# Every matmul of the inner loop on 64x32 tiles of the array, row halves summed on VectorE, and two score slots for three

## The chip, the core and the metric

The kernel runs on one core of a Trainium2 chip. The metric is the device time in microseconds; a kernel's time is the median of its runs. Beside the timed runs one execution was profiled, and all durations below come from that one.

The engines are PE (TensorE, matrix products; PEld is its loading of weights), DVE (VectorE), ACT (ScalarE), POOL (GpSimd) and SP (which here issues most DMAs). Each works through its own list of instructions in order and waits for the others by semaphores.

## The reference

Two attention layers read the same input and are mixed by a gate. Layer A has 32 query heads over one shared head of keys and values; layer B has 32 full heads. Sequence 2048, model width 512, head width 16, all float32.

```python
g = _sigmoid((x * gate_w).sum(-1, keepdims=True))
# A: q = x@wq in 32 heads; k = x@wk, v = x@wv (one head)
# B: q, k, v = x@wqkv in 32 heads each
scores = einsum("bhqd,bhkd->bhqk", q, k) * (Dh ** -0.5)   # A: "bhqd,bkd->bhqk"
p = _softmax(scores, axis=-1)
o = einsum("bhqk,bhkd->bhqd", p, v)                        # A: "bhqk,bkd->bhqd"
layer = o.transpose(...).reshape(B, S, D) @ wo
return g * a + (1 - g) * b
```

## The kernel before, in words

**Groups and blocks.** The heads are taken in eight groups of eight heads, A and B in turn. A group has two halves of 1024 queries. A half has four passes `s`; a pass treats four blocks at once (two heads by two query blocks of 512) and runs over 16 key chunks `c` of 128. One block of one chunk is a 128x512 tile of scores, keys on the rows. One step of the main loop is one chunk of one pass: four blocks. There are 1024 steps and 2048 activations, each over two blocks.

**A step.** `scores(u)` makes two blocks on PE into one slot of two PSUM banks (`sc`, three slots), fp16 operands split into high and low parts stacked on 64 rows, so each block is a 64x128 tile of the array and two run side by side. ACT takes the exponential of the 128x1024 slot into `pr`. `values(m)` multiplies `pr` with the values (float32, 128x32 tiles, four blocks side by side on the four column strips) and sums over the 16 chunks in one PSUM bank `aux[turn]`. A column of ones beside the values gives the softmax denominators. A float32 product shows as two matmuls in the trace. After chunk 15 the bank is copied to `raw` by DVE, DMAs spread it into `oT` (sums) and `dT` (denominators), the turn flips, and the other bank of `aux` takes the next pass.

**Side work.** The bank that is not being summed into (`aux[1 - turn]`) serves for all other products, in parts that are slipped into the steps: projections of the next groups' queries and keys (`project`, units of 12 parts; a part is one `by_tiles` call, four matmuls 128*32 over 512 columns), B's values (`v_units`), and the output projection (`o_unit`, three parts for 128 rows of output, added into `acc` by DVE with the gate). `norm_task` (called "a norm" below) divides 128 columns of `oT` by `dT` on DVE: reciprocal, multiplication, and the split into two fp16 parts. Before the loop x is turned and split, and the first projections are made.

**The order.** All instructions are written out by this program, with no scheduler behind it. `_Tasks` decides when side work is issued: `step` runs parts at a rate worked out from each unit's due time, at most about two per step, and issues at most one side function (a norm, a load) per step. In the list of a step stand both `scores`, then `values` of two steps before, then the parts:

```python
for u in range(STEP * j // ACT, STEP * (j + 1) // ACT):
    scores(u)
if j >= 2:
    values(j - 2)
```

Of the kernel before, what the change touches and what calls it, by code (L numbers as in the profile page):

```python
# [10 lines left out]
F32 = mybir.dt.float32  # L11
# [7 lines left out]
P = 128  # L19
# [8 lines left out]
ACT = 2  # L28
STEP = 4
COLS = 32  # L30
SCALE = DH ** -0.5
# [30 lines left out]
class _Tasks:  # L62
# [3 lines left out]
    def __init__(self):  # L66
        self.now, self.credit, self.rest = 0, 0.0, 0
        self.units, self.open, self.side = [], deque(), deque()
        self.moves, self.moved = deque(), 0
# [11 lines left out]
    def _run(self, left):  # L81
        if not self.open:
            for u in self.units:
                if u[0] <= self.now and self.rest <= self.now and len(u[2]) <= 2 * (left - 1):
                    self.units.remove(u)
                    self.open.extend(u[2])
                    break
        if not self.open:
            return False
        self.open.popleft()()  # L90
        if not self.open:
            self.rest = self.now + 1
        return True

    def step(self, left):
        self.now += 1
        if self.side and self.side[0][0] <= self.now and len(self.open) not in (1, 2):
            self.side.popleft()[1]()
        if self.moves and self.moved <= self.now - 3:
            self.moved = self.now  # L100
            self.moves.popleft()()
        n = len(self.open)
        rate = n / max(1, left - 1)
        for u in self.units:
            n += len(u[2]) + 1
            rate = max(rate, n / max(1, u[1] - self.now))
        self.credit = min(self.credit + rate, 2.2)
        while self.credit >= 1.0 and self._run(left):
            self.credit -= 1.0

    def finish(self):
        while self.open:
            self.open.popleft()()
        self.rest = self.now + 1

    def flush(self):

        assert not self.moves
        self.rest = 0
        ahead = 0  # L120
        while self.open or self.units or self.side:
            if self.side and ahead < 2 and not (self.units and not ahead):
                self.side.popleft()[1]()
                ahead += 1
                continue
            ahead -= ahead > 0
            self.now += 100
            self._run(1 << 20)
            self.finish()
            self.rest = 0  # L130

# [10 lines left out]
def _fast(ctx, tc, x, wq_a, wk_a, wv_a, wo_a, wqkv_b, wo_b, gate_w, out, flag):  # L142
# [11 lines left out]
    turn = [0]  # L154

    xT = cst.tile([P, 2, NK, S], F16, name="xT")
# [11 lines left out]

    def by_tiles(out, lhsT, rhs, start, stop):

        for n in range(0, P, COLS):
            nc.tensor.matmul(out[n : n + COLS], lhsT[:, n : n + COLS], rhs, start=start, stop=stop)  # L172

# [87 lines left out]
    def x_unit(t):  # L261
        return [lambda: x_one(t, aux[1 - turn[0]])]

# [4 lines left out]
    def kv_products(b, i, bank):  # L268
        m = 2 * DH + 1
        pk = bank()[:, : 4 * m].rearrange("p (a b) -> p a b", a=4)  # L270
# [12 lines left out]
        nc.vector.tensor_scalar(vA[:, 4 * b : 4 * b + 4, :DH], pk[:, :, DH : 2 * DH], UP ** -2, None, op0=ALU.mult)  # L283
        nc.vector.tensor_copy(z[:, 4 * b : 4 * b + 4], pk[:, :, 2 * DH])
        nc.vector.tensor_scalar(k32, k32, -QK_MAX, None, op0=ALU.max)
        split(kn[:, :, 0, 0, :], kn[:, :, 0, 2, :], k32)
        nc.vector.tensor_copy(kn[:, :, 0, 1, :], kn[:, :, 0, 0, :])
        nc.vector.tensor_copy(kn[:, :, 0, 3, :], kn[:, :, 0, 2, :])
        nc.vector.tensor_copy(kn[:, :, 1], kn[:, :, 0])
        absmax("k_a", b, k32, AX.XY)  # L290
        kns[b] = kn

    def k_turned(b, bank):
        pkt = bank()[:, : 2 * P].bitcast(F16)
        for i in range(4):
# [4 lines left out]
    def kv_units(b):  # L300
        spare = lambda: aux[1 - turn[0]]
        return [lambda i=i: kv_products(b, i, spare) for i in range(4)], [lambda: k_turned(b, spare)]


    def project(w, needs, name, kind, n0, half, parts, put, queues, late=None):
# [15 lines left out]
        def product(i, c, a, b, first, last):  # L321
            assert needs in ready
            if first:
                if i == 0:
                    state["hi"] = ops.tile([P, 2, BLK], F16, tag="hi", name=f"hi{name}{half}")
                    state["lo"] = ops.tile([P, 2, BLK], F16, tag="lo", name=f"lo{name}{half}")
                state["ps"] = aux[1 - turn[0]]
            at = (2 * half + i) * BLK
# [3 lines left out]
            y = ops.tile([P, BLK], F32, tag="y", name=f"y{name}{half}{i}")  # L332
            nc.vector.tensor_scalar(y, state["ps"], UP ** -2, QK_MAX, op0=ALU.mult, op1=ALU.min)  # L333
            nc.vector.tensor_scalar(y, y, -QK_MAX, None, op0=ALU.max)
            split(state["hi"][:, i], state["lo"][:, i], y)
# [33 lines left out]
    def v_units(gi):  # L369
        w, state = weights["b", gi, "v"], {}  # L370

        def product(t, part):
            assert ("v", "b", gi) in ready
            a, b = PARTS[part]
            if t % 4 == 0 and part == 0:
                state["ps"] = aux[1 - turn[0]].rearrange("p (t a b d) -> p t a b d", t=4, a=4, b=2)
            ps = state["ps"]
            for c in range(NK):
                by_tiles(ps[:, t % 4].rearrange("p a b d -> p (a b d)"),
                         xT[:, a, c, t * P : (t + 1) * P], w[:, b, c * P : (c + 1) * P],  # L380
# [3 lines left out]
            for hh in range(2):  # L384
                nc.vector.tensor_scalar(vB[:, t - 3 : t + 1, :, 2 * hh, :], ps[:, :, :, hh, :], UP ** -2, None,  # L385
                                        op0=ALU.mult)
            if t == NT - 1:
# [9 lines left out]
    def o_unit(src, gi, t, o16, last):  # L397
        w, i, state = weights[src, gi, "o"], "ab".index(src), {}

        def product(part):  # L400
            assert ("o", src, gi) in ready
            a, b = PARTS[part]
            if part == 0:
                state["ps"] = aux[1 - turn[0]]
# [4 lines left out]
            if (src, gi) == ("a", 0):  # L409
                nc.vector.tensor_scalar(acc[:, t], state["ps"], g, None, op0=ALU.mult)  # L410
            else:
                nc.vector.scalar_tensor_tensor(acc[:, t], state["ps"], g, acc[:, t], op0=ALU.mult, op1=ALU.add)  # L412
            if last:
# [29 lines left out]
    first_w[1]()  # L443
    x_pair(4)
    x_pair(6)
    late = []
# [6 lines left out]
    for i in range(4):  # L453
        kv_products(0, i, lambda: aux[0])
    k_turned(0, lambda: aux[0])
    x_pair(8)
    x_one(10, aux[1])
    x_one(11, aux[0])
    for f in late:
# [22 lines left out]
    def scores(u):  # L482
        todays = blocks[ACT * u : ACT * (u + 1)]
        sc = ps_s.tile([P, ACT, BLK], F32, tag="sc", name=f"sc{u}")
        for i, (n, half, _, c, p, j, hh) in enumerate(todays):
# [3 lines left out]
            r = slice(64 * hh, 64 * hh + 64)  # L489
            nc.tensor.matmul(sc[:, i], k[r, c * P : (c + 1) * P],  # L490
                             Q[src, gi, half, p][r, j * BLK : (j + 1) * BLK], start=True, stop=True)
        probs[u] = prob.tile([P, ACT, BLK], F32, tag="pr", name=f"pr{u}")
# [3 lines left out]
    def values(m):  # L496
# [4 lines left out]
        if c == 0 and m:  # L501
            todo.finish()
            turn[0] ^= 1
        o = aux[turn[0]]
        for i, (_, _, _, _, p, j, hh) in enumerate(quad):
            assert src == "a" or ("v", gi) in ready
            v = vA[:, c, :] if src == "a" else vB[:, c, p, hh : hh + 2, :].rearrange("p a d -> p (a d)")
            at = 4 * m + i
            nc.tensor.matmul(o[32 * i : 32 * i + 32, :], v, probs[at // ACT][:, at % ACT],  # L509
                             start=c == 0, stop=c == NT - 1)  # L510
# [3 lines left out]
        nc.vector.tensor_copy(raw, o)  # L514
        if s == 0:
# [73 lines left out]


    turn[0] = 1
    steps = len(blocks) // STEP
# [152 lines left out]
```

## Time and profile before

| what | value |
|---|---|
| median of three runs | 1964.23 us (1963.01 to 1965.0) |
| the profiled execution | 1963.35 us, its span 1961.6 us |
| PE busy | 1908.4 us, 97% |
| ACT busy | 1906.1 us, 97% |
| DVE busy | 559.5 us, 29% |
| granted TensorE clock, mean | 0.994 |

A busy share is a union of records that overlap: PE's matmuls are pipelined, and ACT's records of one activation after another overlap too. So the two 97% say that both engines have something under way nearly always, not which of them sets the pace. The first exponential starts 28.3 us into the span and the last one ends at 1936.9 us. What precedes is the loading and turning of x and the first projections, what follows is the last output projection.

### The profile page before, as it was taken

What the parts mean: (1) busy time and instruction counts of PE and PEld (TensorE: products, weight loads), DVE (VectorE), ACT (ScalarE), POOL (GpSimd) and SP (SyncE); (2) the same over time, 40 slices, a digit from 0 to 9 for tenths busy, and PEclk for the clock granted to TensorE, in tenths of its full rate; (3) what the DMA queues carried; (4) which work ended last, traced back from release to release, by engine and by line L of the source; (5) the groups of instructions that cost most, each with busy time, mean ns of one, the idle gap of its engine ahead of it and who ended that gap; (6) DMA issues with size and microseconds to landing.
All of it is one profiled execution on the core that took longest, in us unless ns stands there. A gap on an engine that the chain in (4) does not pass through costs nothing.

```text
span 1961.6 us, 46364 instructions
## 1 busy us (share of the span) xinstructions
PE 1908.4 (97%) x19472; PEld 517.5 (26%) x19472; DVE 559.5 (29%) x1093; ACT 1906.1 (97%) x2071; POOL 92.7 (5%) x103
## 2 busy tenths in 40 slices
PE   7999999999999999999999999999999999999997
PEld 4222322222222232222222233222222223222221
DVE  4225042141322414123142332412314241241414
ACT  4999999999999999999999999999999999999995
POOL 5001000200000100020000100002000000000000
PEclk8999999999999999999999999999999999999998
DMA  4022100101011110110101210011100111001012
GB/s 142 7 48 50 31 12 15 47 12 33 7 33 47 33 27 7 31 36 11 29 12 31 59 33 14 12 33 28 27 19 17 34 41 32 12 12 28 6 29 82
DMA packets 55416, 59.82 MB, mean 30 GB/s; under 512 B 21440, under 2 KB 29632, under 8 KB 55200
## 3 DMA queue, kind: packets, MB, share of 16 engines
q1 hardware_dynamic: 53984, 55.66, 11.9%
q8 instruction: 155, 2.54, 0.6%
q0 software_dynamic: 528, 0.69, 0.1%
q14 instruction: 61, 0.50, 0.1%
q10 hardware_dynamic: 688, 0.43, 0.1%
HBM read 10.55 MB, written 4.19 MB: 8 GB/s over the span
## 4 chain that ended last, share of the span: by engine, by line
PE 63%; ACT 18%; issue 13%; DVE 5%; SPq 1%; DMA 0%; ACTq 0%; DVEq 0%
PE aux L509 32%; PE sc L490 19%; ACT pr L494 18%; PE aux L172 11%; DVE dTa L425 1%; DVE stats L176 1%; SPq L316 0%; DMA acc<-in_A_x_dram 0%; DVE lob L180 0%; DVE acc L412 0%; DVE xT L247 0%; SPq L525 0%; DVE yb L333 0%; DVE rawb L514 0%; PE aux L275 0%
## 5 line engine op out<-in xcount | busy, mean ns | idle before, releaser
L494 ACT ACTIVATE pr<-sc 128x1024 f32<-128x1024 f32 x2048 | 1895.2, 1261 | 10.5 <-PE sc L490 6.5
L509 PE MATMUL aux<-pr,vA 128*32 128x512 f32 x4096 | 546.3, 605 | 0.0
L509 PE MATMUL aux<-pr,vB 128*32 128x512 f32 x4096 | 545.5, 605 | 0.0
L490 PE MATMUL sc<-Qb,K 64*128 64x512 f16 x2048 | 359.8, 383 | 18.0
L490 PE MATMUL sc<-Qa,kA 64*128 64x512 f16 x2048 | 319.8, 382 | 3.7 <-ACT pr L494 0.2
L490 PEld LDWEIGHTS <-K 64*128 64x128 f16 x2048 | 99.8, 93 | 466.6 <-issue 464.0
L412 DVE SCALAR_TENSOR_TENSOR acc<-aux,gate_up,acc 128x512 f32<-128x512 f32 x112 | 84.0, 750 | 437.4 <-PE aux L172 437.4
L490 PEld LDWEIGHTS <-kA 64*128 64x128 f16 x2048 | 71.0, 94 | 258.4 <-issue 243.9
L509 PEld LDWEIGHTS aux<-pr,vA 128*32 128x32 f32 x4096 | 80.6, 108 | 197.4 <-issue 195.1
L509 PEld LDWEIGHTS aux<-pr,vB 128*32 128x32 f32 x4096 | 80.9, 108 | 128.5 <-issue 122.2
L172 PE MATMUL aux<-w16ob,o16b 128*32 128x512 f16 x768 | 69.2, 392 | 8.3 <-DVE acc L412 6.0
L172 PEld LDWEIGHTS <-xT 128*32 128x32 f16 x3072 | 55.5, 97 | 63.9 <-issue 63.9
L172 PE MATMUL aux<-xT,w16qb 128*32 128x512 f16 x768 | 66.2, 379 | 3.8 <-DVE rawb L514 2.2
L172 PE MATMUL aux<-w16oa,o16a 128*32 128x512 f16 x768 | 68.6, 379 | 0.1
L172 PE MATMUL aux<-xT,w16qa 128*32 128x512 f16 x768 | 65.8, 379 | 1.3 <-DVE ya L333 0.9
L385 DVE TENSOR_SCALAR vB<-aux 128x256 f32<-128x256 f32 x32 | 12.1, 420 | 181.9 <-PE aux L172 181.9
L425 DVE RECIPROCAL dTb<-dTb 128x128 f32<-128x128 f32 x64 | 60.5, 946 | 10.0 <-DMA dTb<-rawb 9.8
L425 DVE RECIPROCAL dTa<-dTa 128x128 f32<-128x128 f32 x64 | 60.5, 945 | 7.9 <-DMA dTa<-rawa 7.9
L172 PE MATMUL aux<-w16vb,xT 128*32 128x128 f16 x3072 | 61.8, 219 | 0.7 <-DVE rawa L514 0.7
L333 DVE TENSOR_SCALAR yk<-aux 128x512 f32<-128x512 f32 x16 | 11.1, 692 | 176.6 <-PE aux L172 176.6
L172 PE MATMUL aux<-xT,w16kb 128*32 128x512 f16 x768 | 60.9, 379 | 0.0
L333 DVE TENSOR_SCALAR ya<-aux 128x512 f32<-128x512 f32 x16 | 11.1, 692 | 170.6 <-PE aux L172 170.6
(119 smaller groups left out, 598.9 us busy)
## 6 DMA issues: line engine op xcount, KB each, us to landing
acc<-in_A_x_dram SPq DMA_DIRECT2D x16, 256.0 KB, 6.0
oTa<-rawa SPq DMA_DIRECT2D x128, 32.0 KB, 1.9
dTa<-rawa SPq DMA_DIRECT2D x128, 32.0 KB, 2.0
K<-hik SPq DMA_DIRECT2D x128, 32.0 KB, 1.9
K<-lok SPq DMA_DIRECT2D x128, 32.0 KB, 1.9
Qb<-hib SPq DMA_DIRECT2D x128, 32.0 KB, 1.9
Qb<-lob SPq DMA_DIRECT2D x128, 32.0 KB, 2.0
out_dram<-acc SPq DMA_DIRECT2D x16, 256.0 KB, 2.1
```

The costliest lines, as they stand in the source:

```text
L172: nc.tensor.matmul(out[n : n + COLS], lhsT[:, n : n + COLS], rhs, start=start, stop=stop)
L176: nc.vector.tensor_reduce(stats[:, n, i : i + 1], src, axis=axis, op=ALU.max, apply_absolute_value=True)
L333: nc.vector.tensor_scalar(y, state["ps"], UP ** -2, QK_MAX, op0=ALU.mult, op1=ALU.min)
L385: nc.vector.tensor_scalar(vB[:, t - 3 : t + 1, :, 2 * hh, :], ps[:, :, :, hh, :], UP ** -2, None, op0=ALU.mult)
L412: nc.vector.scalar_tensor_tensor(acc[:, t], state["ps"], g, acc[:, t], op0=ALU.mult, op1=ALU.add)
L425: nc.vector.reciprocal(d, d)
L490: nc.tensor.matmul(sc[:, i], k[r, c * P : (c + 1) * P], Q[src, gi, half, p][r, j * BLK : (j + 1) * BLK], start=True, stop=True)
L494: nc.scalar.activation(probs[u][:, :m], sc[:, :m], AF.Exp, scale=SCALE / (UP * UP))
L509: nc.tensor.matmul(o[32 * i : 32 * i + 32, :], v, probs[at // ACT][:, at % ACT], start=c == 0, stop=c == NT - 1)
```

## The change

1. Tiles of 64 rows x 32 columns for scores, values and projections alike. A block of scores is four matmuls instead of one; a value product or a projection is split into its upper and lower 64 rows, each half summed in a bank of its own. So `aux` becomes two pairs of banks.
2. Where a sum leaves PSUM, DVE reads two banks: `added` is one operation that scales the first bank into SBUF and one that adds the second. `o_unit` accumulates twice.
3. PSUM has eight banks; with four for `aux`, the `sc` slots go from three to two.
4. The order of a step: first slot of scores, parts, second slot of scores, `values` of one step before (not two), side functions. Parts run two per step as soon as a unit may start, in place of the rate from due times.

```diff
-COLS = 32
+ROWS, COLS = 64, 32
+MOST = 2
...
-                if u[0] <= self.now and self.rest <= self.now and len(u[2]) <= 2 * (left - 1):
+                if u[0] <= self.now and self.rest <= self.now and len(u[2]) <= MOST * (left - 1):
...
-    def step(self, left):
+    def products(self, left):
+
         self.now += 1
+        for _ in range(MOST):
+            self._run(left)
+
+    def others(self):
         if self.side and self.side[0][0] <= self.now and len(self.open) not in (1, 2):
             self.side.popleft()[1]()
-        if self.moves and self.moved <= self.now - 3:
+        if self.moves and self.moved <= self.now - 2:
...
-    ps_s = ctx.enter_context(tc.tile_pool(name="ps_s", bufs=3, space=PSUM))
+    ps_s = ctx.enter_context(tc.tile_pool(name="ps_s", bufs=2, space=PSUM))
...
-    aux = [ps_x.tile([P, BLK], F32, name=f"aux{i}") for i in range(2)]
+    aux = [[ps_x.tile([P, BLK], F32, name=f"aux{n}{i}") for i in range(2)] for n in range(2)]
...
-    def by_tiles(out, lhsT, rhs, start, stop):
+    def by_tiles(outs, lhsT, rhs, start, stop):
 
         for n in range(0, P, COLS):
-            nc.tensor.matmul(out[n : n + COLS], lhsT[:, n : n + COLS], rhs, start=start, stop=stop)
+            for i, out in enumerate(outs):
+                r = slice(ROWS * i, ROWS * (i + 1))
+                nc.tensor.matmul(out[n : n + COLS], lhsT[r, n : n + COLS], rhs[r], start=start, stop=stop)
+
+    def added(dst, outs, scale):
+
+        nc.vector.tensor_scalar(dst, outs[0], scale, None, op0=ALU.mult)
+        nc.vector.scalar_tensor_tensor(dst, outs[1], scale, dst, op0=ALU.mult, op1=ALU.add)
...
-            nc.vector.tensor_scalar(y, state["ps"], UP ** -2, QK_MAX, op0=ALU.mult, op1=ALU.min)
-            nc.vector.tensor_scalar(y, y, -QK_MAX, None, op0=ALU.max)
+            added(y, state["ps"], UP ** -2)
+            nc.vector.tensor_scalar(y, y, QK_MAX, -QK_MAX, op0=ALU.min, op1=ALU.max)
...
-            nc.tensor.matmul(sc[:, i], k[r, c * P : (c + 1) * P],
-                             Q[src, gi, half, p][r, j * BLK : (j + 1) * BLK], start=True, stop=True)
+            for a in range(0, P, COLS):
+                nc.tensor.matmul(sc[a : a + COLS, i], k[r, c * P + a : c * P + a + COLS],
+                                 Q[src, gi, half, p][r, j * BLK : (j + 1) * BLK], start=True, stop=True)
...
-            nc.tensor.matmul(o[32 * i : 32 * i + 32, :], v, probs[at // ACT][:, at % ACT],
-                             start=c == 0, stop=c == NT - 1)
+            for a, o in enumerate(aux[turn[0]]):
+                r = slice(ROWS * a, ROWS * (a + 1))
+                nc.tensor.matmul(o[32 * i : 32 * i + 32, :], v[r], probs[at // ACT][r, at % ACT],
+                                 start=c == 0, stop=c == NT - 1)
...
-        nc.vector.tensor_copy(raw, o)
+        added(raw, aux[turn[0]], 1.0)
...
-    for j in range(steps + 2):
+    for j in range(steps + 1):
         if j < steps:
             if blocks[STEP * j][2:] == (0, 0, 0, 0, 0):
                 begin(*blocks[STEP * j][:2])
-            for u in range(STEP * j // ACT, STEP * (j + 1) // ACT):
-                scores(u)
-        if j >= 2:
-            values(j - 2)
+            scores(2 * j)
         for f in early.get(j, ()):
             f()
-        todo.step(-(j - 1) % NT if j >= 2 else NT)
+        todo.products((1 - j) % NT + 1 if j > 1 else NT)
+        if j < steps:
+            scores(2 * j + 1)
+        if j:
+            values(j - 1)
+        todo.others()
     todo.flush()
```

How this moves instructions is shown at three places around the end of one pass of group B. The names: `K01` and `Qb001` are keys and queries of B, `sc`, `pr`, `vB` as above, `w16qb0` a weight of the query projection, `xT` the turned input, `o16a01` the normalized output of the group before, `aux0`, `aux1` the two banks before and `aux00` to `aux11` the two pairs after.

PE, before: the second score slot of a step, then the values of two steps earlier, then a part.

```order
L490 MATMUL sc299_4477<-Qb001_2570,K01_1713 128x512
L509 MATMUL aux0_82<-pr294_4443,vB_91 32x512 x2
L509 MATMUL aux0_82<-pr295_4448,vB_91 32x512 x2
L172 LDWEIGHTS w16qb0_439
L172 MATMUL aux1_83<-xT_84,w16qb0_439 32x512
```

PE, after, the first step in which parts may use the pair that the last pass has left: the end of the first score slot (8 matmuls), and the parts right behind it.

```order
L495 LDWEIGHTS K01_2555
L495 MATMUL sc292_8338<-Qb001_4618,K01_2555 32x512
L169 LDWEIGHTS o16a01_7836
L169 MATMUL aux10_84<-w16oa0_109,o16a01_7836 32x512
L169 LDWEIGHTS o16a01_7836
L169 MATMUL aux11_85<-w16oa0_109,o16a01_7836 32x512
```

Behind these stand 14 more such matmuls, then the 8 of the step's second slot `sc293`, then the 8 value products of `pr290` and `pr291`, then `sc294`. So the parts now stand ahead of the second slot of their own step, and a slot is written again after one other slot instead of two.

DVE, before, at the end of that pass: the query projection leaves PSUM in one operation, a norm (four rows), and the sums of the pass leave PSUM in one operation.

```order
L333 TENSOR_SCALAR yb010_4368<-aux0_82 128x512
L334 TENSOR_SCALAR yb010_4368<-yb010_4368 128x512
L179 TENSOR_SCALAR hib01_4163<-yb010_4368 128x512
L180 SCALAR_TENSOR_TENSOR lob01_4164<-yb010_4368,hib01_4163 128x512
L176 TENSOR_REDUCE stats_88<-yb010_4368 128x1
L425 RECIPROCAL dTa01_2460<-dTa01_2460 128x128
L426 SCALAR_TENSOR_TENSOR oTa01_2459<-oTa01_2459,dTa01_2460 128x128
L431 CAST o16a01_4183<-oTa01_2459 128x128
L432 TENSOR_TENSOR o16a01_4183<-oTa01_2459,o16a01_4183 128x128
L514 COPY rawb000_4406<-aux1_83 128x512
```

DVE, after, the first half of the same projection and the first of five norms that follow it; behind the fifth stands the second half, `yb011`.

```order
L173 TENSOR_SCALAR yb010_7810<-aux00_82 128x512
L174 SCALAR_TENSOR_TENSOR yb010_7810<-aux01_83,yb010_7810 128x512
L336 TENSOR_SCALAR yb010_7810<-yb010_7810 128x512
L181 TENSOR_SCALAR hib01_7562<-yb010_7810 128x512
L182 SCALAR_TENSOR_TENSOR lob01_7563<-yb010_7810,hib01_7562 128x512
L178 TENSOR_REDUCE stats_90<-yb010_7810 128x1
L429 RECIPROCAL dTa01_4661<-dTa01_4661 128x128
L430 SCALAR_TENSOR_TENSOR oTa01_4660<-oTa01_4660,dTa01_4661 128x128
L435 CAST o16a01_7836<-oTa01_4660 128x128
L436 TENSOR_TENSOR o16a01_7836<-oTa01_4660,o16a01_7836 128x128
```

DVE, after, behind the second half `yb011`: a norm, the two accumulations of one output unit, a norm, and the sums of the pass.

```order
L429 RECIPROCAL dTa01_4661<-dTa01_4661 128x128
L430 SCALAR_TENSOR_TENSOR oTa01_4660<-oTa01_4660,dTa01_4661 128x128
L435 CAST o16a01_7836<-oTa01_4660 128x128
L436 TENSOR_TENSOR o16a01_7836<-oTa01_4660,o16a01_7836 128x128
L414 TENSOR_SCALAR acc_87<-aux00_82,gate_up_97 128x512
L416 SCALAR_TENSOR_TENSOR acc_87<-aux01_83,gate_up_97,acc_87 128x512
L429 RECIPROCAL dTa01_4661<-dTa01_4661 128x128
L430 SCALAR_TENSOR_TENSOR oTa01_4660<-oTa01_4660,dTa01_4661 128x128
L435 CAST o16a01_7836<-oTa01_4660 128x128
L436 TENSOR_TENSOR o16a01_7836<-oTa01_4660,o16a01_7836 128x128
L173 TENSOR_SCALAR rawb000_8282<-aux10_84 128x512
L174 SCALAR_TENSOR_TENSOR rawb000_8282<-aux11_85,rawb000_8282 128x512
```

Between two projections there was one norm and are five, and each departure from PSUM is two operations. PE's list grows from 24,997 rows to 69,543.

More of the change, by code (lines that the diff above doesn't have):

```diff
@@ L127, in flush @@
             self.now += 100
-            self._run(1 << 20)
-            self.finish()
-            self.rest = 0
+            while self._run(1 << 20) and self.open:
+                pass
 def _sigmoid(nc, gate, z, scale):
@@ L261, in x_unit @@
     def x_unit(t):
-        return [lambda: x_one(t, aux[1 - turn[0]])]
+        return [lambda: x_one(t, spare()[t % 2])]
     PARTS = ((0, 0), (0, 1), (1, 0))
@@ L300, in kv_units @@
     def kv_units(b):
-        spare = lambda: aux[1 - turn[0]]
-        return [lambda i=i: kv_products(b, i, spare) for i in range(4)], [lambda: k_turned(b, spare)]
+        return ([lambda i=i: kv_products(b, i, spare()[0]) for i in range(4)],
+                [lambda: k_turned(b, spare()[1])])
     def project(w, needs, name, kind, n0, half, parts, put, queues, late=None):
@@ L326, in product @@
                     state["lo"] = ops.tile([P, 2, BLK], F16, tag="lo", name=f"lo{name}{half}")
-                state["ps"] = aux[1 - turn[0]]
+                state["ps"] = spare()
             at = (2 * half + i) * BLK
@@ L384, in product @@
             for hh in range(2):
-                nc.vector.tensor_scalar(vB[:, t - 3 : t + 1, :, 2 * hh, :], ps[:, :, :, hh, :], UP ** -2, None,
-                                        op0=ALU.mult)
+                added(vB[:, t - 3 : t + 1, :, 2 * hh, :],
+                      [bank.rearrange("p (t a b d) -> p t a b d", t=4, a=4, b=2)[:, :, :, hh, :] for bank in ps],
+                      UP ** -2)
             if t == NT - 1:
@@ L403, in product @@
             if part == 0:
-                state["ps"] = aux[1 - turn[0]]
+                state["ps"] = spare()
             by_tiles(state["ps"], o16[:, a], w[:, b], part == 0, part == 2)
@@ L408, in product @@
             g = gate_up[:, i, t : t + 1]
[L409 to L412, printed above, removed]
+            for n, bank in enumerate(state["ps"]):
+                if (src, gi, n) == ("a", 0, 0):
+                    nc.vector.tensor_scalar(acc[:, t], bank, g, None, op0=ALU.mult)
+                else:
+                    nc.vector.scalar_tensor_tensor(acc[:, t], bank, g, acc[:, t], op0=ALU.mult, op1=ALU.add)
             if last:
@@ L443, in _fast @@
     first_w[1]()
-    x_pair(4)
-    x_pair(6)
+    for t in range(4, 8):
+        x_one(t, aux[t // 2 % 2][t % 2])
     late = []
@@ L501, in values @@
         if c == 0 and m:
-            todo.finish()
+            assert not todo.open
             turn[0] ^= 1
-        o = aux[turn[0]]
         for i, (_, _, _, _, p, j, hh) in enumerate(quad):
```

35 lines of the change are left out of this document (12 added, 23 removed).

## The prediction

> **What bounds the kernel now.** I read the page first: who is busy, and which groups carry it.
>
> ```profile
> span 1961.6 us, 46364 instructions
> PE 1908.4 (97%) x19472; PEld 517.5 (26%) x19472; DVE 559.5 (29%) x1093; ACT 1906.1 (97%) x2071; POOL 92.7 (5%) x103
> PE 63%; ACT 18%; issue 13%; DVE 5%; SPq 1%; DMA 0%; ACTq 0%; DVEq 0%
> L494 ACT ACTIVATE pr<-sc 128x1024 f32<-128x1024 f32 x2048 | 1895.2, 1261 | 10.5 <-PE sc L490 6.5
> L509 PE MATMUL aux<-pr,vA 128*32 128x512 f32 x4096 | 546.3, 605 | 0.0
> L172 PE MATMUL aux<-w16oa,o16a 128*32 128x512 f16 x768 | 68.6, 379 | 0.1
> ```
>
> PE and ACT are both at 97%, so the averages don't decide. The pace does: activations of line 494 in two kinds of stretches and in the whole loop (third number: busy us, x: activations).
>
> ```profile
> 74.00:1934.00 1860.00, 1853.45 (x2006) 1.00 0.12 27
> 300.00:540.00 240.00, 240.00 (x263) 1.00 0.10 23
> 680.00:730.00 50.00, 49.58 (x54) 1.00 0.15 33
> ```
>
> With one activation cut by each edge, 300 to 540 gives 240/262 = 0.916 us, the loop 1860/2005 = 0.928, and 680 to 730, where B's values are projected, 50/53 = 0.94. I take 0.916 as ACT's own pace, since ACT never stopped in that stretch: a step of two activations can't be under 1.832 us. The loop lies 0.012 x 2006 = 24 us above it. What holds it there shows in the chain of waits at 703 us, where a step is 1.98 us and all of it PE:
>
> ```profile
> 703.86 0.45 PE aux L172 x32
> 704.31 0.54 PE sc L490 x4
> 704.85 0.99 PE aux L509 x8
> ...
> 1931.90 0.22 PE aux L172 x4
> ```
>
> So one core has two bounds: ACT's 1.832 in most steps, PE in those with much side work.
>
> **Part 1, the tiles.** Four products of 512 columns cost 0.22 together, so a score step of four, two at a time, should be 2 x 0.215 = 0.43 and is 0.54. A float32 pass outlasts an fp16 one by 605 - 379 = 226 ns, so it streams about 0.43, and two passes should be 0.87 where 0.99 stands. The 0.11 and 0.12 stand exactly where the tile's shape changes, and 128*32 products behind 128*32 values have none. With one shape I take them as gone: PE needs 0.43 + 0.87 + 0.45 = 1.75 in the fullest step, under 1.832. The gain is then the whole 24 us; its other end is 0, if the 0.23 stays. Twice as many matmuls, each on half the rows, stream equally long if eight run at once, as four do now.
>
> **Part 2, two slots and the new order.** When a wait ends late in front of a score slot, ACT feels it. The nearest rows are these, at the end of a pass:
>
> ```profile
> 782.35 0.94 DVE L425 RECIPROCAL dTa<-dTa 128x128 f32<-128x128 f32 x1
> ...
> 784.12 0.68 DVE L514 COPY rawb<-aux 128x512 f32<-128x512 f32 x1
> ...
> 784.86 0.61 PE L172 MATMUL aux<-xT,w16qb 128*32 128x512 f16 x8 [0.66 <-DVE rawb L514]
> ...
> 785.40 0.60 PE L490 MATMUL sc<-Qb,K 64*128 64x512 f16 x4
> ...
> 785.89 2.86 ACT L494 ACTIVATE pr<-sc 128x1024 f32<-128x1024 f32 x3 [0.39 <-PE sc L490]
> ```
>
> DVE is busy with a norm (782.35 to 784.12, 1.77 us), the copy of the sums comes behind it, a part on PE waits 0.66 for it, the scores queue behind the part, and ACT stands 0.39. From scores to activation are 0.49; three activations last 2.86, so one alone takes 2.86 - 2 x 0.916 = 1.03 from start to end.
>
> Now the new step, with t = 0 where PE starts the second slot, just after an activation has freed it. Scores to 0.215, values to 1.085, then the next step's first slot to 1.30, two parts to 1.73; the second slot's turn is at 1.832. PE's room is 0.10. The slot scored from 1.085 has its activation start at 1.085 + 0.49 + 0.04 (six more matmuls to issue at 7 ns, half of the 14 ns of 0.45/32) = 1.615. To keep ACT's pace it must start 1.03 - 0.916 = 0.11 before the previous one ends (at 1.79), at 1.68. Room: 0.06. So the two slots suffice in the plain step, and ACT loses what a wait of a part exceeds 0.16.
>
> **Part 3, two banks to leave.** The rows that price DVE (mean ns behind busy us):
>
> ```profile
> 779.50 0.69 DVE L333 TENSOR_SCALAR yb<-aux 128x512 f32<-128x512 f32 x1 [2.17 <-PE aux L172]
> ...
> L412 DVE SCALAR_TENSOR_TENSOR acc<-aux,gate_up,acc 128x512 f32<-128x512 f32 x112 | 84.0, 750 | 437.4 <-PE aux L172 437.4
> L385 DVE TENSOR_SCALAR vB<-aux 128x256 f32<-128x256 f32 x32 | 12.1, 420 | 181.9 <-PE aux L172 181.9
> ...
> L247 DVE SCALAR_TENSOR_TENSOR xT<-aux,xT 128x512 f16<-128x512 f32 x6 | 4.0, 688 | 8.5 <-ACT xT L246 8.5
> ```
>
> `added` is 0.69 + 0.69 (a second operand from PSUM, as L247) = 1.38 where 0.69 stood. A projection's chain on DVE, 2.85 now (779.50 to 782.35), becomes 3.54; an output unit's accumulation goes from 0.75 to 1.50, a quarter of B's values from 2 x 0.42 to 4 x 0.42. None of this bounds DVE, which is at 29%. But the bank pair must be empty before the next unit, and the parts now come at full rate. A unit's last part ends at 1.73; with 0.17 to drain and 0.05 to hand over, DVE starts at 1.95. The next unit's part wants to start at 1.832 + 1.30 = 3.13. What follows, wait less 0.16:
>
> - *Projection, DVE free:* 1.95 + 1.38 + 0.06 = 3.39, wait 0.26, loss 0.1; about 32 times: 3 us.
> - *Projection with five norms ahead* (the order on DVE, 8 times): 3.54 + 5 x 1.77 = 12.39 of DVE work between two departures that PE places six steps (10.99) apart. DVE is 1.40 late, the wait 1.66, the loss 1.5: 12 us.
> - *The sums `raw` after that:* on DVE stand the chain, a norm, an accumulation, a norm: 1.40 + 3.54 + 1.77 + 1.50 + 1.77 = 9.98 after the projection was ready. PE finishes the pass four steps later, at 4 x 1.832 - 0.64 + 1.5 = 8.19. So 1.79 late; 1.79 + 1.38 + 0.06, less the 1.82 until the next part, is a wait of 1.41 and a loss of 1.2. The order has it (with small variations) at the 15 half-groups after the first: 18 us.
> - *Accumulations behind norms elsewhere,* six places at about the same: 7 us.
> - *Output units in a row:* a lone third part ends at 1.52, two accumulations later it is 3.30, wait 0.17, at the edge of the room; I take 0.1, some 72 times: 7 us.
> - *B's values:* 1.97 + 4 x 0.42 + 0.06 = 3.71, wait 0.58, loss 0.4, 15 times: 6 us.
>
> Together 53 us. These sums are as good as the room of 0.16: with 0.5 of room they would be about 30, with none about 75. In the row above, with three slots and one operation, the same wait of 0.66 cost 0.39.
>
> **Part 4, ends.** Before the loop one more departure from PSUM (0.69) is in the chain, and parts of the first ten steps now stand between two slots: +1 (0 to +4). Behind it:
>
> ```profile
> 1938.03 0.69 DVE rawb L514
> ...
> 1949.72 1.50 PE aux L172 x12
> 1951.25 0.76 DVE acc L412
> ```
>
> The last `raw` costs 0.69 more and each of the last four output units 0.75 more, 3.7; but five older units that now precede them are done inside the loop, which starts the last norms some 2 to 3 us sooner: +1 (-3 to +4). The parts moved from every third step to every second (`moves`) issue DMAs on SP, which nobody in the loop's chain waits for: 0.
>
> **The sum.** The profiled execution took 1963.35 us, 0.9 below the median. 1963.35 - 24 + 53 + 1 + 1 = 1994.4; I say 1995, slower by 1.6%.
>
> **Rivals.**
>
> *The room is larger or the norms come earlier (faster).* DVE runs ahead of PE: a norm waits only for its data, and if the six steps between two departures stretch a little, the norms are done before the next one. For it: DVE is at 29%. Against it: seven such stops are in the trace already. It decides where the waits fall under 0.16; without them 1963.35 - 24 + 2 = 1941, with a third of them about 1957.
>
> *The room of 0.06 isn't there.* If the values still take 0.99, the first slot is 0.06 late once in two steps: +500 x 0.06 = 30, 2025. Against it, a product behind values of the same shape shows no gap.
>
> *PE can't issue so fast.* A step with B's values takes 64 pairs of load and matmul. The trace shows 14 ns a pair (0.45/32); 64 in 0.45 need 7. At 14 they take 0.90, and 96 such steps grow from 1.83 to 2.2: +35, 2030. On such a floor the Trainium skill ("TensorE: Matmul & The Clock Gate", the section on 56 against 53.3 ns) says that matmuls start no closer than about 25 ns, however short. By that rule, as an estimate, these 96 steps would take 2.9 us and the sum be near 2098; the row of 14 ns contradicts it, though not for eight tiles.
>
> *Eight float32 tiles don't run at once.* Three rounds of 0.43 in place of two put the first slot 0.37 late in every second step: +500 x 0.37 = 185, 2180. The Trainium skill (same page, "Measured speedup vs the span model") has packed tiles cost some 4 ns each; by that the values would be 0.02 longer, inside the room. No row shows eight.
>
> **How the numbers follow.** The sum's case 0.51, the faster rival 0.21, the missing room 0.11, the issue 0.11, the rounds 0.06. The predicted time is the first's, 1995, whose own range is 1970 to 2015 (room 0 to 0.5, ends). Taking in the faster rival down to 1940 and the two at 2025 and 2030, the range is 1940 to 2035. About 0.2% (4 us) is what a measurement tells from no change: faster 0.21, same 0.06 (the edges of the first two cases), slower 0.73.
>
> **What would show it.** Right: scores of 0.43 and values of 0.87 in the chain, without gaps at the change from one to the other; ACT's pace at 0.916 in plain stretches and in those with B's values; some thirty stops of ACT over 1 us, each behind a part that waits for DVE's `raw`, `y` or `acc`, with a norm ahead of it on DVE. Wrong: a step over 1.832 without any wait for DVE, or the 64 pairs over 0.45, or no stop over 0.5.

## The result and the profile after

The kernel after takes 2097.2 us (median of four runs, 2096.16 to 2099.7) against 1964.6 before: ratio 1.068, interval 1.066 to 1.070, 132.6 us slower. The prediction was 1995, its range ended at 2035. The direction was right, the size was not: 31 us slower were forecast, and about half of what was measured came from a wait that the forecast's sum did not hold.

The page of after, with the groups that answer to those shown of before:

```profile
span 2097.8 us, 101649 instructions
PE 1824.2 (87%) x46864; PEld 844.2 (40%) x46864; DVE 747.4 (36%) x1365; ACT 1926.7 (92%) x2071; POOL 93.1 (4%) x103
q8 instruction: 369, 6.05, 1.2%
ACT 46%; PE 23%; DVE 16%; issue 13%; SPq 2%; DMA 1%; DVEq 0%; ACTq 0%; POOL 0%
L499 ACT ACTIVATE pr<-sc 128x1024 f32<-128x1024 f32 x2048 | 1915.9, 1060 | 117.4 <-PE sc L495 107.1
L169 PE MATMUL aux<-w16vb,xT 64*32 64x128 f16 x6144 | 90.1, 220 | 41.7 <-issue 34.4
```

PE went from 97% to 87%, ACT from 97% to 92%: neither is the bound throughout any more. Line 499 now stands idle for 117.4 us, nearly all of it waiting for scores (10.5 before), and PE itself waits for "issue" in front of B's value projections, that is, for nothing the profile shows. Activations in three stretches (busy us, count, clock, DMA share, GB/s):

```profile
300.00:330.00 30.00, 29.95 (x34) 1.00 0.06 13
400.00:460.00 60.00, 59.57 (x65) 1.00 0.14 35
703.00:736.00 33.00, 23.62 (x25) 1.00 0.16 36
```

The first two keep ACT's pace. In the third, where B's values are projected, 25 activations fill 33 us: 24 x 0.916 = 21.98 would do, so 11.0 are lost in twelve steps. The chain of waits in between shows what PE does when nothing stops it:

```profile
707.87 0.24 PE aux L169 x5
708.11 0.21 PE sc L495 x8
708.33 0.86 PE aux L515 x16
709.18 0.22 PE sc L495 x8
709.40 0.57 PE aux L169 x64
```

Values take 0.86, the two slots of scores 0.21 and 0.22, and no gap stands between the shapes: what Part 1 of the prediction said of the tiles. 64 pairs of load and matmul take 0.57, 9 ns a pair; Part 1 had 0.45 for these parts, so the fullest step needs 1.86 of PE and not 1.75, 0.03 over ACT's pace, some 3 us in 96 steps. Yet a few microseconds to either side PE stops in the middle of such a row of 64. The timeline:

```profile
705.73 0.80 PE L169 MATMUL aux<-w16vb,xT 64*32 64x128 f16 x59
...
707.87 0.24 PE L169 MATMUL aux<-w16vb,xT 64*32 64x128 f16 x5 [1.34 <-issue]
...
708.46 2.10 ACT L499 ACTIVATE pr<-sc 128x1024 f32<-128x1024 f32 x2 [1.31 <-PE sc L495]
```

59 of 64 matmuls run, 1.34 us of nothing, then the last five; ACT waits 1.31 behind. The other stretch to look at is a projection that ends with norms ahead of it, in the timeline at 327 us:

```profile
327.56 0.95 DVE L429 RECIPROCAL dTa<-dTa 128x128 f32<-128x128 f32 x1
...
329.34 0.68 DVE L173 TENSOR_SCALAR yb<-aux 128x512 f32<-128x512 f32 x1
330.07 0.37 PE L169 MATMUL aux<-w16oa,o16a 64*32 64x512 f16 x1 [0.71 <-DVE yb L173]
...
330.87 0.62 PE L169 MATMUL aux<-w16oa,o16a 64*32 64x512 f16 x15 [0.42 <-DVE yb L174]
...
331.84 3.01 ACT L499 ACTIVATE pr<-sc 128x1024 f32<-128x1024 f32 x3 [1.26 <-PE sc L495]
```

The norm ends, `added` empties the pair in two operations, the next unit's part waits for the first bank (0.71) and then the second (0.42), and ACT stops for 1.26. That is the stop that the prediction priced at 1.5.

Where the 136.2 us of span went, from the records of line 499 (a step's loss is the time from one second activation's end to the next, less 1.832):

| part of the span | before | after |
|---|---|---|
| until the first activation ends | 29.3 | 35.3 |
| loss in the first ten steps | 8.0 | 8.4 |
| loss in the steps with B's value projections | 9.4 | 79.0 |
| loss in all other steps | 15.2 | 70.9 |
| after the last activation | 24.7 | 28.8 |

In steps with B's values 69.6 came on top of what the kernel before lost, in the other steps 55.7: two sums of similar size, and the experiments take them one by one. The 70.9 are 37 stops over 0.4 us (43.7 together) and 226 small ones (26.0), mostly of 0.16 in every second step of a run of output units.

### The profile page after: what moved, and what is told of

It reads as the page before. It is cut to its first block, busy times and chain, and to the rows that moved or that the text cites. A ratio compares the mean times of both kernels' runs of the same rounds, so it can differ in the third digit from the quotient of the medians.

```text
span 2097.8 us, 101649 instructions
## 1 busy us (share of the span) xinstructions
PE 1824.2 (87%) x46864; PEld 844.2 (40%) x46864; DVE 747.4 (36%) x1365; ACT 1926.7 (92%) x2071; POOL 93.1 (4%) x103
## 4 chain that ended last, share of the span: by engine, by line
ACT 46%; PE 23%; DVE 16%; issue 13%; SPq 2%; DMA 1%; DVEq 0%; ACTq 0%; POOL 0%
ACT pr L499 45%; PE aux L515 9%; PE aux L169 7%; PE sc L495 6%; DVE dTa L429 2%; DVE acc L416 2%; DVE dTb L429 2%; SPq L318 1%; DVE stats L178 1%; DVE oTa L430 1%; DVE o16a L436 1%; DVE o16a L435 1%; DVE oTb L430 1%; DVE yb L174 1%; DVE vB L174 0%
## 5 line engine op out<-in xcount | busy, mean ns | idle before, releaser
L499 ACT ACTIVATE pr<-sc 128x1024 f32<-128x1024 f32 x2048 | 1915.9, 1060 | 117.4 <-PE sc L495 107.1
L515 PE MATMUL aux<-pr,vA 64*32 64x512 f32 x8192 | 570.4, 590 | 5.9 <-issue 5.9
L515 PE MATMUL aux<-pr,vB 64*32 64x512 f32 x8192 | 554.7, 590 | 0.0
L495 PE MATMUL sc<-Qb,K 64*32 64x512 f16 x8192 | 450.8, 380 | 103.3 <-ACT pr L499 102.9
L495 PE MATMUL sc<-Qa,kA 64*32 64x512 f16 x8192 | 467.3, 380 | 44.7 <-ACT pr L499 37.8
L495 PEld LDWEIGHTS <-K 64*32 64x32 f16 x8192 | 208.7, 90 | 498.8 <-issue 459.4
L495 PEld LDWEIGHTS <-kA 64*32 64x32 f16 x8192 | 201.2, 90 | 379.4 <-issue 339.5
L515 PEld LDWEIGHTS aux<-pr,vA 64*32 64x32 f32 x8192 | 166.6, 105 | 38.7 <-issue 16.2
L515 PEld LDWEIGHTS aux<-pr,vB 64*32 64x32 f32 x8192 | 161.4, 105 | 26.7 <-ACT pr L499 1.2
L169 PE MATMUL aux<-w16ob,o16b 64*32 64x512 f16 x1536 | 101.8, 395 | 33.5 <-DVE acc L416 9.9
L169 PE MATMUL aux<-w16oa,o16a 64*32 64x512 f16 x1536 | 99.2, 378 | 18.8 <-DVE yb L173 4.2
```

Source lines behind the costliest of these rows:

```text
L169: nc.tensor.matmul(out[n : n + COLS], lhsT[r, n : n + COLS], rhs[r], start=start, stop=stop)
L495: nc.tensor.matmul(sc[a : a + COLS, i], k[r, c * P + a : c * P + a + COLS], Q[src, gi, half, p][r, j * BLK : (j + 1) * BLK], start=True, s ...
L499: nc.scalar.activation(probs[u][:, :m], sc[:, :m], AF.Exp, scale=SCALE / (UP * UP))
L515: nc.tensor.matmul(o[32 * i : 32 * i + 32, :], v[r], probs[at // ACT][r, at % ACT], start=c == 0, stop=c == NT - 1)
```

## The experiments

Each kernel is the one after with the edit shown. The theories: **A**, PE gets its instructions in blocks of 256, and the next block isn't there in time when 256 are used up too fast; **B**, each pair of load and matmul has a price of about 28 ns whatever its length; **C**, B's values lose by their doubled departure on DVE; **D**, the other stops are parts that wait for DVE.

What spoke for A from the start was a count. PE's matmuls in three stretches of after, cut at moments when PE started again after such a pause (us, PE busy, matmuls, clock, DMA share, GB/s):

```profile
707.87:711.62 3.75, 3.37 (x128) 1.00 0.19 42
711.62:715.64 4.02, 2.47 (x128) 1.00 0.21 47
715.64:719.39 3.75, 2.32 (x128) 1.00 0.17 39
```

From one restart to the next it is 128 matmuls, and with their loads 256 instructions, three times running. The DMA view of 703 to 736 us has the other half:

```profile
q8 instruction: 9, 0.15, 1.9%
```

Nine packets of 16 KB of instructions in 33 us, one per 3.7 us; over the whole kernel 369 packets (the page's row above) for 2 x 46864 = 93728 loads and matmuls, 254 for each. Before, it was this row of its page, for 2 x 19472, 251 for each:

```profile
q8 instruction: 155, 2.54, 0.6%
```

**B's value projections on whole rows** (`e1_v_full`).

```diff
-                by_tiles([bank[...] for bank in ps], xT[...], w[...], ...)
+                for n in range(0, P, COLS):
+                    nc.tensor.matmul(ps[0][n : n + COLS, ...], xT[:, a, c, t * P + n : t * P + n + COLS], w[...], ...)
...
-                added(vB[...], [bank...[:, :, :, hh, :] for bank in ps], UP ** -2)
+                nc.vector.tensor_scalar(vB[...], ps[0]...[:, :, :, hh, :], UP ** -2, None, op0=ALU.mult)
```

> The kernel after, with only B's value projections put back on 128x32 tiles, summed in one bank and taken out by one operation. Theory A (instruction blocks): PE gets its instructions in blocks of 256, and a block is not there before some 3.65 us after the one before it was begun. The 96 steps with B's value projections have 192 instructions (2.74 us) and lose 0.9 each; here they have 128 (1.83 us). So about -73, and the tile's shape changes twice in each of these steps again, +0.14 x 96 = +13: 2037, range 2025 to 2050. Theory B (each load and matmul pair, however short, takes PE 28 ns on the average, 96 pairs in 2.74 us): 64 pairs, 1.8 us, the same number; this run does not tell A from B. Theory C (what costs is VectorE's doubled departure of these values, 0.4 to 0.6 us at 16 units, and the issue gaps are only where PE waits for it): -10 to -15, 2083 to 2090.

Measured: 2025.0 us, 72 less than after, at the edge of the range of A. The steps with B's values lose 14.3 in place of 79.0, 0.15 each, so a step takes 1.98 as at 703 us in the kernel before, where the shape changes twice too. The other steps lose 63.9 in place of 70.9, with eight stops over 0.4 fewer. C falls: its 10 to 15 us are not what was lost. A and B stand.

**Redundant weight loads** (`e3_ldw`).

```diff
+        for i in range(0 if todo.open or u < 40 else 40):
+            a = i % 4 * COLS
+            nc.tensor.ldweights(k[r, c * P + a : c * P + a + COLS], tile_position=(64 * hh, a))
```

> The kernel after, with 40 redundant weight loads (64x32, nothing multiplied with them) behind each score slot that has no side work open: 46120 loads in all, about 576 steps' worth, no matmul more, the result unchanged. Theory A (blocks of 256 instructions, 3.65 us each at the least): a plain step has 64 + 80 = 144 instructions, 2.05 us in place of 1.832; +0.22 x 576 = +127, less where a step has them in one slot only: 2200, range 2175 to 2230, and a plain stretch such as 400 to 430 us shows steps of 2.05. Theory B (a price per matmul): no matmul is added, 2097 to 2105. If the loads themselves take PE's time (14 ns for a load and a matmul in the trace, so 7 for a load, 0.56 a step, PE 1.30 + 0.56 = 1.86): 2097 + 0.03 x 576 = 2114.

Measured: 2570.6 us. Every theory missed, since the price of a load was wrong. Its timeline, at a slot with 40 loads:

```profile
400.47 0.64 PEld L499 LDWEIGHTS <-K 64*32 64x32 f16 x39
...
403.75 0.17 PEld L499 LDWEIGHTS <-K 64*32 64x32 f16 x17
```

39 loads take 0.64, and with the last one's own 0.09 taken off that is some 15 ns each and not 7. It is no fixed price: the second row has 5 ns each, and of the 1153 slots with loads 534 took 14 to 16 ns a load, 353 took 26 to 28 and 180 took 4.6. What decides between them was not tried. One slot at 15 and one at 27 are 1.7 us of loads in a step on top of 1.3, and PE becomes the bound. So the plain steps, for which the run was made, tell nothing of A and B.

**Scores cut into quarters** (`e9_quarters`), the same question without time on the array.

```diff
+            w = BLK
+            if u >= 40 and not todo.open and (n < 4 or u // 2 % 4 == 0):
+                w = BLK // 4
+            for q in range(0, BLK, w):
-                nc.tensor.matmul(sc[a : a + COLS, i], k[...], Q[...][r, j * BLK : (j + 1) * BLK], ...)
+                    nc.tensor.matmul(sc[a : a + COLS, i, q : q + w], k[...], Q[...][r, j * BLK + q : j * BLK + q + w], ...)
```

> A repair of the run with redundant loads, without time on the array: the kernel after, with each score matmul of 512 columns cut into four of 128 where no side work is open, which streams the same columns and gives the same result with four times as many instructions. In the first four groups in every such step (196 steps of 160 instructions, 173 with one slot cut), in the last four only in every fourth step (60 and 38). Theory A (blocks of 256, 3.65 us each, two blocks of room): where cut steps follow each other a step takes 160/256 x 3.65 = 2.28 us, +0.45 x 196 and about 0.1 to 0.2 x 173 for the half-cut ones beside side work: +88 to +125; a lone cut step among plain ones (160 + 3 x 64 in four steps) costs nothing: 2205, range 2180 to 2225. Theory B (a price of 28 ns for each load and matmul pair): 80 pairs take 2.28 in each cut step, lone or not: as A in the first half, and +0.45 x 60 more in the second, where a 2.28 would stand in every fourth plain step: 2215 to 2250. If only streaming counts: 2097.

Measured: 2235.4 us, above A's range and inside B's. The total doesn't decide, the places do. Activations in a stretch of steps that are all cut, and in one where every fourth is:

```profile
394.00:474.00 80.00, 63.29 (x67) 1.00 0.10 25
1510.00:1570.00 60.00, 60.00 (x66) 1.00 0.11 29
```

In the first, 67 activations fill 80 us, 2.42 a step; in the second ACT never stops (60/65 = 0.923). Compared step by step with after, the 196 fully cut steps in a row lost 92.4 us more, 0.47 each (A and B both said 0.45); the 60 lone ones lost 0.08 each, and 0.05 in the step behind, where B wanted 0.45. So 160 instructions in a step cost little when the steps around have 64, 0.13 in two steps: B falls. The packets of instructions in the two stretches:

```profile
q8 instruction: 21, 0.34, 1.9%
```

```profile
q8 instruction: 11, 0.18, 1.3%
```

One per 3.8 us where PE starves, one per 5.5 us where it doesn't. What A left out was the steps around: the half-cut ones lost 19 us, inside the 17 to 35 that were expected, but the uncut steps of the first half lost 14 more and those of the second half 9.

**B's value projections at one part a step** (`e6_v_one`): the same work and the same instructions, thinner, and begun earlier in the pass.

```diff
+                    self.slow = u[3] and len(u[2]) <= left - 1
...
-        for _ in range(MOST):
-            self._run(left)
+        for i in range(MOST):
+            if not i or not self.slow or not self.open:
+                self._run(left)
...
-                todo.add(v_units(nxt[1]), now + 22, due + 10)
+                for i, unit in enumerate(v_units(nxt[1])):
+                    todo.add([unit], now + (4 if n else 22), (now+20+16*i+16*(i>1)) if n else due + 10, True)
```

> The kernel after, with B's value projections at one part a step in place of two where the rest of the pass has room for it: 144 steps with one part and 24 with two, in place of 96 with two. The tiles, the instructions and the departures on VectorE are those of after; only their density changes, 128 instructions in most of these steps in place of 192. Theory A (blocks of 256 instructions, 3.65 us each at the least): 128 instructions need 1.83 us, just ACT's pace, so only the 24 dense steps lose 0.9: -57, and some waits at the end of units fall on other places: 2030, range 2020 to 2050. Theory C (the departures on VectorE cost the time): the same number of departures, 2085 to 2097.

Measured: 2038.6 us, 59 less than after. The steps with B's values lose 27.1 in place of 79.0, and 22 of these in the steps that stayed dense, for which A has 22. Three stops of 4.2 to 5.1 us at the start of a group of heads are new in this run (at 782, 1274 and 1769 us): at 782 PE waited for the DMA of B's queries, which now came late, and the granted clock was 0.50 for 3.4 to 6.8 us around each. Without them the gain would have been larger.

**The norm's last operations on GpSimd** (`e4_norm_pool`).

```diff
-            nc.vector.scalar_tensor_tensor(o, o, UP, d, op0=ALU.mult, op1=ALU.mult)
...
+                nc.gpsimd.tensor_tensor(o, o, d, op=ALU.mult)
+                nc.gpsimd.tensor_scalar(o, o, UP, None, op0=ALU.mult)
...
-                nc.vector.tensor_copy(o16[:, 0], o)
-                nc.vector.tensor_sub(o16[:, 1], o, o16[:, 0])
+                eng.tensor_copy(o16[:, 0], o)
+                eng.tensor_sub(o16[:, 1], o, o16[:, 0])
```

`eng` is GpSimd, but for the last half group. The multiplication, one operation on DVE, becomes two on GpSimd.

> The kernel after, with three of the four steps of a norm on GpSimd (multiplication, rounding, remainder); VectorE keeps the reciprocal, 0.95 in place of 1.77 us a norm. Theory D (the stops of 1.2 to 1.4 us outside the stretches with B's values are parts that wait for VectorE with norms ahead): at five norms ahead VectorE has 3.54 + 5 x 0.95 = 8.3 us of work for 10.99 us, so the eight stops at the projections go, and those at the sums behind them mostly: about 26 stops, -30 to -40, 2060. Theory E (the doubled departure itself makes the stops, or GpSimd slows VectorE at the shared memory): 2085 to 2110.

Measured: 2066.2 us, 31 less. Outside B's values 13 stops over 0.4 remain of 37, 13.7 us of 43.7; inside, nothing changed (81.9). Its timeline at the projection that stopped ACT at 331.84 in after, an operation of a norm on GpSimd and the projection's departure:

```profile
327.49 0.53 POOL L434 TENSOR_SCALAR oTa<-oTa 128x128 f32<-128x128 f32 x1
327.71 0.69 DVE L173 TENSOR_SCALAR yb<-aux 128x512 f32<-128x512 f32 x1 [3.38 <-PE aux L169]
```

DVE has been idle for 3.38 us and waits for PE, not the other way round. D holds for these stops.

**One step more of pause between units** (`e5_rest`).

```diff
-            self.rest = self.now + 1
+            self.rest = self.now + 2
```

> The kernel after, with one step more of pause between two units of side work (self.rest = self.now + 2). Theory D (VectorE has not emptied the pair of banks when the next unit begins): the 0.16 us lost in every second step of a run of output units (about 130 such steps) go, and so do the waits of 0.1 to 0.6 at the end of projections and of B's values: -20 to -32, 2065 to 2077. The stops behind norms stay. If these 0.16 are only ACT catching up after a stop, and not waits of their own: 2090 to 2098. Theory A says nothing against either: the instructions per step within a unit stay the same.

Measured: 2065.0 us, 32 less. The small losses outside B's values (and the pauses between their units) went from 26.0 to 1.8. So the 0.16 are waits of their own, for the pair of banks of the unit before, and not ACT catching up. The stops behind norms stayed, and the units that moved made some worse; the timeline, where a part waits 2.58 for `raw`:

```profile
336.15 0.58 PE L169 MATMUL aux<-w16oa,o16a 64*32 64x512 f16 x1 [2.58 <-DVE rawb L173]
...
338.56 1.02 ACT L499 ACTIVATE pr<-sc 128x1024 f32<-128x1024 f32 x1 [3.77 <-PE sc L495]
```

The 3.77 of ACT is not the wait for `raw` alone: behind PE's pause the granted clock was 0.50 from 335.8 to 342.6 us, and the scores that follow last 1.05 for eight, against 0.59 behind the same stop in after. This run has four such stretches inside the loop, 20.5 us together; after has one of 3.4, near its end.

**All remedies together** (`e8_best`): `e1_v_full`, `e4_norm_pool` and `e5_rest`, and outside the loop one bank at a time:

```diff
+    def pair():
+        alone[0] ^= 1
+        return spare()[alone[0] :][:1] if alone[1] else spare()   # alone[1]: before and behind the loop
...
+            if len(outs) == 1:
+                nc.tensor.matmul(outs[0][n : n + COLS], lhsT[:, n : n + COLS], rhs, start=start, stop=stop)
+                continue
```

> Four remedies together: B's value projections on 128x32 tiles (measured alone: -72), the norm's last three operations on GpSimd (-31), one step more of pause between units (-32), and before the loop and behind it projections and output units on 128x32 tiles in one bank, the two banks of a pair by turns (estimate: -2 to -6). Scores, values and side work in the loop stay on 64x32 tiles with two score slots. If the causes are separate, as theories A and D have it: 2097 - 72 - 31 - 32 - 4 = 1958, range 1950 to 1970, that is level with the kernel before or a little faster. If two of the remedies take away the same loss: 1975 to 2000.

Measured: 1959.7 us over eleven runs (1957.2 to 1965.2), 0.9987 of the kernel before, interval 0.9978 to 0.9996: the same within 2%, as the sum of the separate remedies said (1958). The causes are separate. Its page:

```profile
span 1957.3 us, 95342 instructions
PE 1771.2 (90%) x43636; PEld 805.1 (41%) x43636; DVE 626.6 (32%) x966; ACT 1900.7 (97%) x2071; POOL 296.4 (15%) x583
L516 ACT ACTIVATE pr<-sc 128x1024 f32<-128x1024 f32 x2048 | 1890.0, 1077 | 15.4 <-PE sc L512 12.1
```

ACT is at 97% again with PE at 90%: what 64x32 tiles save on PE is there, but little of it reaches the time. From the first activation's end to the last one's it is 1905.8 us against 1907.6 before, 1.8 less, because the loop of before had only 24 to give and the steps with B's values, back on whole rows, keep 11.4 of loss (pauses between their units counted in). Another 3.0 are gained behind the loop (21.7 against 24.7), where the units are on whole rows as before, and 0.5 is lost ahead of it.

## Why the prediction was wrong

**The step that failed** is the last sentence of Part 1: twice as many matmuls "stream equally long". They do, in 0.86 and 0.21. But they are also twice as many instructions, and these come in packets by a queue of their own. I priced the count only as time that PE takes to issue, in the rival "PE can't issue so fast", at 14 ns a pair and 35 us. The place was right (the 96 steps with B's values), the chance was 0.11, the mechanism was another and its price double: 192 instructions a step at 256 per 3.65 us (the median distance of two packets in these stretches is 3.68) are 2.74 us, 0.9 over the pace and 87 us in 96 steps; 79.0 were lost there. It is shown by taking instructions away (e1), by thinning them (e6) and by adding them elsewhere (e9). What sets the 3.65 stays open. Two of the prediction's own signs of being wrong came with it: steps over 1.832 without a wait for DVE, and 64 pairs in 0.57, over 0.45. The 9 ns a pair also answer the rival's 14: the time to issue alone is worth the 3 us above. The packets stood in the profile of before, 155 of 16 KB for 38944 loads and matmuls; dividing the two gives 251, close to the 256, and 192 a step would have meant one packet per 2.44 us, where the loop of before never had two packets closer than 4.5 (behind the loop there is one distance of 3.3). That would have warned of a rate not seen before; it does not show where the limit lies.

The Trainium skill ("Runtime: NRT & Kernel Launch", "Instruction fetch mechanics") has instructions refilled in blocks of 16 KiB, 256 instructions, fetched while the current one runs. The trace agrees with the block. The page also says that the cost of crossing a block is mostly hidden; here it is hidden at about 128 instructions in a step of 1.83 us, and not at 160 or 192 where such steps follow each other.

The prediction gave 2098 as an estimate by the Trainium skill's rule of 25 ns between matmuls ("TensorE: Matmul & The Clock Gate", the section on 56 against 53.3 ns). The measured 2097 isn't that rule's: 64 pairs run in 0.57 between two stops, and a lone step with 80 pairs costs 0.08.

**Right, and nearly to size.** The stops by DVE: the eight projections behind norms at 1.5 each, 12 us; in the steps' losses there are nine of 1.36 or 1.37 and one of 0.43, 12.7. The sums `raw` behind them, 15 at 1.2, 18 us: eleven stand outside B's values, at 1.23 to 1.80, 14.5 together, and the others fall in the steps with B's values. Accumulations elsewhere, six places, 7 us: 1.25, 1.26 and 1.26 in the middle, 0.95, 2.12 and 1.22 near the end, 8.1 (at the 2.12 the granted clock was 0.50 for 3.4 us). The other ten stops of the 37, 8.4 us, stand at the edges of the stretches with B's values. ACT's pace of 0.916 in plain stretches, the scores at 0.43 for both slots, eight float32 tiles at once: all as said.

**Mis-sized.** Output units in a row were put at 0.1 in 72 places, 7 us; they lose 0.16 in some 130 steps, and with the other small waits 26 us (e5 takes away 24). Their room in the step was at the edge, and I took the middle of it. The ends were put at +2: they are +10.6. Before the loop +6.0: x lands 0.8 us later by the median of its DMAs and the first projection takes 0.43 a part in place of 0.23 before the two departures are even counted. These were different from run to run: the first activation started between 30.9 and 34.3 us in the runs of the kernels that share this code (in the run with 30.9, `e6_v_one`, the same projection takes 0.22 a part), and why was not tried. Behind the loop +4.1: the 3.7 of the departures came. The norms did start sooner, 6.4 us behind the last activation in place of 9.2, but GpSimd began its part of the first one 3.1 us after its input was there, in place of 0.1, and PE waited 2.47 for it; why GpSimd was late stays open.

Summed up: the 47 of waits outside B's values became 71, the 2 of the ends (with the first ten steps) became 11, and the 6 at B's values became 79, most of it waiting for instructions (46 pauses of 1.27 are 58), which the sum did not have. The gain by the shapes seems to be there where nothing else stops PE: outside B's values and the first ten steps, the kernel before lost 12.7 us in 116 small losses (0.02 to 0.4 each), the one with all remedies 2.4 in 19. But the two differ in the order of a step and in the pauses as well, and no run changed the shape alone.

## What to carry to other kernels

Count instructions per microsecond, not only the time that they keep the array: when a change multiplies small matmuls, divide the packets of the instruction queue into PE's instructions, and compare the rate in the densest stretch with the highest that the trace has sustained. Here a single step of 160 instructions cost 0.13 us with the step behind it and a row of them 0.47 each, so spreading dense work over more steps is a remedy. And where two units share a pair of banks, one step more of pause between them took away nearly all of the small waits.

## What the runs showed of the hardware

- PE's instructions came in packets of 16 KB, one per 256. Where PE ran short, 46 pauses of over 0.7 us from one start to the next (1.27 on the average) in after, and 123 (of 1.18) in `e9_quarters`, stand at exactly the same place when loads, matmuls and PE's semaphore rows are counted by 256; 51 in `e3_ldw`, 44 of them in its steps with B's values, stand there too. The packet began 2.4 and 2.6 us (medians, after and `e9_quarters`) before PE went on, the next one 1.15 us after. The shortest distance of two packets was 3.3 us in either, and 3.0 in any run.
- That the distance is about the same at 36 GB/s of other traffic (703 to 736 us of after) and at 25 (394 to 474 us of `e9_quarters`) speaks against contention as its cause, but no run changed the traffic by itself.
- A weight load that no matmul uses, on four tiles of one half of the rows, took 14 to 16 ns in most slots, 26 to 28 in others and 4.6 in the rest, while a load and its matmul of 128 columns took 9 ns together, on eight tiles.
- GpSimd did four operations of 128x128 of a norm in place of three on DVE without making DVE's slower: `added` took 0.69 and 0.69 beside them.
- Behind a pause of PE of 2.6 us (`e5_rest`, 336 us) the granted clock was 0.50 for 6.8 us. Behind the pauses of 1.3 us at the instruction packets no such row stands in after.
